# Two pads shift the upper half of the on-chip memory map so that matmul operands start at multiples of 128 bytes

## The chip, the cores and the metric

The kernel runs on one core of a Trainium2 chip. The metric is the device time of one execution in microseconds (us). The kernel before takes 2042.87 us, the median of 3 runs (2042.85 to 2042.97).

## The reference

Three layers follow each other; each one's output is the next one's input.

```
# attention: softmax of q over the head dimension, of k over the sequence
kv = einsum('bhsd,bhse->bhde', softmax_seq(k), v)          # 4 batches, 8 heads, 576 x 64
x  = einsum('bhsd,bhde->bhse', softmax_dim(q), kv)         # -> 2304 tokens x 512
# first MLP, float64 weights
h = x @ w_in; x = maximum(0.01*h, h) @ w_out               # 512 -> 2048 -> 512
# eight experts, every token through all of them
P = exp(x @ w_gate - max); 8 rounds of row and column normalization   # 2304 x 8
out = sum_e P[:, e] * (maximum(x @ w1[e], 0) @ w2[e])      # 512 -> 1024 -> 512
```

## The kernel before

**Numbers.** Matmul operands of the two MLPs are float32 values kept as two `fp32r` parts, a high one and a low one. Each product is three matmuls, high*high, high*low, low*high, summed in PSUM. The helper `mm` (line 178 in the profile) issues them all. Every matmul is paired with its own weight load: one operand (the second argument of `mm`, the stationary one, 128 x 128) is loaded into the array by LDWEIGHTS, the other (the third argument, the moving one, 384 or 512 columns) is streamed through it.

**First MLP** (functions `first` and `second`): four phases `ph` of 24 steps each, six token blocks of 384 by four weight units. One step is a `first` (tile `ph`, 12 matmuls of 384 columns: stationary weights, moving `xs`) and a `second` (tiles `y0` to `y3`, 12 matmuls of 384 columns: stationary weights, moving `hh`). In phases 0 and 2 the weights lie in tile `wa`, in phases 1 and 3 in tile `wb_t`. After a block's fourth unit, VectorE adds `y` into `acc` (line 217); the next `second` writes the same PSUM banks. Attention work is interleaved into the time before the first MLP and into its phase 0.

**Experts** (functions `group`, `product`, `y_tile`): 96 groups. Each runs seven products of six matmuls with 384 columns (tiles `pa` to `pd`: stationary `wa`, moving `xs`), and three output tiles of 12 matmuls with 512 columns (tile `e`: stationary the hidden activations, which lie in `xs`; moving the second weights, which lie in `wb_t`). The first two groups have no output tiles, and two more after the last group have nothing else, so there are 96 sets of 36 such matmuls.

**What sets the order.** Python code writes out the order of all engines (a manual schedule with the tables at `at(...)`); the change touches none of it.

**Where tiles lie.** Tiles are placed one behind the other, every size rounded up to 32 bytes per partition. Pools on the left grow upward from byte 16512, which follows a scratch area and four small constants. Pools with `side="right"` grow downward from byte 229344. The table gives the start of each tile that a matmul reads, as the allocation places it, per partition, before and after the change:

| tile | read by | bytes | start before | mod 128 | start after | mod 128 |
|---|---|---|---|---|---|---|
| `ident`, `ones` | attention transposes, column sums | 512 | 16512, 17024 | 0 | same | 0 |
| `acc` (6) | attention | 6144 | 18816 and on | 0 | same | 0 |
| `xs` | moving in `ph`, `p*`; stationary in `e` | 79872 | 55680 | 0 | same | 0 |
| `wa` | stationary in `ph`, `y`, `p*` | 32768 | 135552 | 0 | same | 0 |
| `hh` (2) | moving in `y` | 3072 | 168416, 171488 | 96 | 168448, 171520 | 0 |
| `wb_t` | stationary in `ph`, `y`; moving in `e` | 32768 | 196576 | 96 | 196480 | 0 |
| `kv` (2) | attention | 2048 | 200288, 202336 | 96 | 200192, 202240 | 0 |
| `k`, `v`, `ke` | attention | 2304, 2560, 2560 | 204384 and on | 96 | 204288 and on | 0 |

Inside these tiles every operand starts at a multiple of 128 bytes from the tile's start, except the gate's weights in `wa` (48 matmuls, in steps of 64 bytes). Besides, 19 small matmuls of the balancing stage read `mrow`, `mall` and `cs`, which start at other multiples of 32 before and after. Tiles that no matmul reads move too: `raw`, `pair`, `ca` and `s` from 32 to 64 mod 128, the small attention and balance statistics by 32 or 96 bytes, and `g`, `c1`, `c2` with `hh` from 96 to 0.

The 96 comes from `mrow`, `mall` and `mneg`: three tiles of 4 bytes in pool `const`, 32 bytes each, in front of pool `h`. On the right side the pools hang from 229344, which is itself 96 mod 128.

Of the kernel before, what the change touches and what calls it, by code (L numbers as in the profile page):

```python
# [8 lines left out]
F32 = mybir.dt.float32  # L9
# [6 lines left out]
P = 128  # L16
# [6 lines left out]
def kernel(  # L23
# [51 lines left out]
    const = ctx.enter_context(tc.tile_pool(name="const", bufs=1))  # L75
# [23 lines left out]

    wa = const.tile([P, PU * US], F32R, name="wa")  # L100

    ml = ml_ctx.enter_context(tc.tile_pool(name="ml", bufs=2))
    att = att_ctx.enter_context(tc.tile_pool(name="att", bufs=2, side="right"))

# [697 lines left out]
```

## Time and profile before

| what | value |
|---|---|
| median of 3 runs | 2042.87 us |
| profiled execution: its time | 2042.97 us |
| its span, first to last instruction | 2041.2 us |
| TensorE (PE) matmul busy | 2007.7 us, 98% |
| weight loads (PEld) busy | 1824.1 us, 89% |
| VectorE (DVE) busy | 1294.8 us, 63% |
| ScalarE (ACT) busy | 806.2 us, 39% |
| GpSimd (POOL) busy | 485.9 us, 24% |
| matmul instructions | 10323 |

The time outside the span is 2042.97 - 2041.2 = 1.77 us. In the span, attention alone fills about the first 55 us, the first MLP runs to about 521 us (phase 0 to about 190, phases 1, 2 and 3 of about 105 to 125 us), and the experts take the rest. The granted clock of TensorE has a mean of 0.992 of full speed. A matmul's duration in the profile is longer than its pitch, the distance from its start to the next one's start, because matmuls are pipelined: durations of successive matmuls overlap. Where matmuls follow without a wait, the pitch is what the time is made of.

### The profile page before, as it was taken

What the parts mean: (1) busy time and instruction counts of PE and PEld (TensorE: products, weight loads), DVE (VectorE), ACT (ScalarE), POOL (GpSimd) and SP (SyncE); (2) the same over time, 40 slices, a digit from 0 to 9 for tenths busy, and PEclk for the clock granted to TensorE, in tenths of its full rate; (3) what the DMA queues carried; (4) which work ended last, traced back from release to release, by engine and by line L of the source; (5) the groups of instructions that cost most, each with busy time, mean ns of one, the idle gap of its engine ahead of it and who ended that gap; (6) DMA issues with size and microseconds to landing.
All of it is one profiled execution on the core that took longest, in us unless ns stands there. A gap on an engine that the chain in (4) does not pass through costs nothing.

```text
span 2041.2 us, 26341 instructions
## 1 busy us (share of the span) xinstructions
PE 2007.7 (98%) x10323; PEld 1824.1 (89%) x10323; DVE 1294.8 (63%) x1941; ACT 806.2 (39%) x1367; POOL 485.9 (24%) x476
## 2 busy tenths in 40 slices
PE   6999999999999999999999999999999999999999
PEld 5899999998889889988998899889888988898887
DVE  8746534335786666666766666666686666666663
ACT  6654323224443333333444333333344333333331
POOL 2324313200223223122132231221322312313220
PEclk8999999999999999999999999999999999999999
DMA  6502111100212212112132122121212221212210
GB/s 228 175 1 83 43 41 42 52 1 0 83 42 83 83 42 83 67 58 83 42 114 83 42 83 69 56 83 44 80 64 92 83 75 50 83 49 76 83 42 31
DMA packets 65452, 138.55 MB, mean 68 GB/s; under 512 B 4656, under 2 KB 4656, under 8 KB 65328
## 3 DMA queue, kind: packets, MB, share of 16 engines
q1 hardware_dynamic: 65328, 136.87, 19.5%
q8 instruction: 81, 1.33, 0.3%
q14 instruction: 43, 0.35, 0.1%
HBM read 132.14 MB, written 4.72 MB: 67 GB/s over the span
## 4 chain that ended last, share of the span: by engine, by line
PE 73%; DVE 1%; ACT 0%; issue 0%; DVEq 0%; ACTq 0%
PE e L178 39%; PE pc L178 10%; PE pd L178 10%; PE pa L178 10%; PE pb L178 5%; DVE wa L446 0%; PE y L178 0%; DVE xs L555 0%; ACT wa L445 0%; DVE pm L387 0%; DVE cs L388 0%; PE pt L178 0%; PE pcs L178 0%; PE pg L178 0%; DVE rs L386 0%; DVE rs L384 0%
## 5 line engine op out<-in xcount | busy, mean ns | idle before, releaser
L178 PE MATMUL e<-wb_t,xs 128*128 128x512 f32 x3456 | 822.4, 395 | 0.0
L178 PEld LDWEIGHTS e<-wb_t,xs 128*128 128x128 f32 x3456 | 647.3, 188 | 148.6
L452 POOL TENSOR_TENSOR s<-pair 128x256 f32<-128x256 f32 x96 | 73.8, 769 | 1207.2 <-DMA pair<-in_w 631.6
L548 DVE SCALAR_TENSOR_TENSOR acc<-e,pm,acc 128x512 f32<-128x512 f32 x264 | 193.2, 744 | 105.7 <-PE e L178 103.0
L178 PE MATMUL pa<-xs,wa 128*128 128x384 f32 x1152 | 231.9, 335 | 0.0
L555 DVE SCALAR_TENSOR_TENSOR xs<-c,xs 128x384 fp32r<-128x384 f32 (+1 forms) x192 | 185.8, 986 | 72.6 <-ACT xs L554 72.6
L178 PE MATMUL pc<-xs,wa 128*128 128x384 f32 x1152 | 230.8, 334 | 0.0
L178 PE MATMUL pd<-xs,wa 128*128 128x384 f32 x1152 | 230.6, 334 | 0.0
L554 ACT ACTIVATE xs<-c 128x768 fp32r<-128x768 f32 x192 | 126.7, 681 | 242.0 <-PE e L178 221.5
L178 PEld LDWEIGHTS pa<-xs,wa 128*128 128x128 f32 x1152 | 203.3, 188 | 8.5
L178 PEld LDWEIGHTS pd<-xs,wa 128*128 128x128 f32 x1152 | 202.4, 188 | 0.1
L178 PEld LDWEIGHTS pc<-xs,wa 128*128 128x128 f32 x1152 | 202.4, 188 | 0.2 <-issue 0.2
L196 DVE TENSOR_TENSOR hh<-g,hh 128x384 fp32r<-128x384 f32 x96 | 58.7, 611 | 208.3 <-ACT g L195 208.3
L446 DVE TENSOR_TENSOR wa<-s,wa 128x768 fp32r<-128x768 f32 x96 | 91.9, 957 | 101.7 <-ACT wa L445 101.6
L445 ACT CAST wa<-s 128x768 fp32r<-128x768 f32 x96 | 80.2, 835 | 168.8 <-POOL s L455 148.2
L570 DVE TENSOR_TENSOR c<-c 128x384 f32<-128x384 f32 x96 | 54.2, 564 | 134.4 <-ACT c L590 134.4
L580 ACT COPY c<-pa 128x384 f32<-128x384 f32 x96 | 46.1, 480 | 212.3 <-PE pa L178 196.9
L194 ACT ACTIVATE hh<-ph 128x384 fp32r<-128x384 f32 x96 | 47.2, 491 | 191.0 <-PE y L178 180.3
L446 DVE TENSOR_TENSOR wa<-pair,wa 128x1024 fp32r<-128x1024 f32 x96 | 120.8, 1258 | 2.6 <-ACT wa L445 2.5
L446 DVE TENSOR_TENSOR wb_t<-pair,wb_t 128x1024 fp32r<-128x1024 f32 x96 | 114.1, 1224 | 8.5 <-PE y L178 4.7
L178 PE MATMUL y<-hh,wb_t 128*128 128x384 f32 x576 | 111.8, 343 | 4.5 <-DVE acc L217 4.2
L455 POOL TENSOR_TENSOR s<-pair,s 128x256 f32<-128x256 f32 x96 | 114.2, 1190 | 7.5
(117 smaller groups left out, 2519.5 us busy)
## 6 DMA issues: line engine op xcount, KB each, us to landing
pair<-in_w SPq DMA_DIRECT2D x192, 512.0 KB, 5.0
raw<-in_wm SPq DMA_DIRECT2D x32, 512.0 KB, 3.8
v<-in_vt SPq DMA_DIRECT2D x16, 320.0 KB, 5.3
k<-in_kt SPq DMA_DIRECT2D x16, 288.0 KB, 5.5
out<-acc SPq DMA_DIRECT2D x18, 256.0 KB, 2.0
acc<-in_q SPq DMA_DIRECT2D x5, 768.0 KB, 6.1
acc<-in_q SPq DMA_DIRECT2D x3, 256.0 KB, 6.8
wg_t<-in_wg SPq DMA_DIRECT2D x1, 16.0 KB, 5.3
```

What stands on the lines that cost most here:

```text
L178: nc.tensor.matmul(o, a, b, start=start, stop=stop, **more)
L194: nc.scalar.activation(hh[:, 0, :], p, AF.Prelu, alpha=0.01)
L196: nc.vector.tensor_tensor(hh[:, 1, :], g, r32(hh[:, 0, :]), op=ALU.subtract)
L445: nc.scalar.copy(hi, a)
L446: return lambda: nc.vector.tensor_tensor(lo, a, r32(hi), op=ALU.subtract)
L452: nc.gpsimd.tensor_tensor(s[:, 0], a21, a22, op=ALU.add)
L455: nc.gpsimd.tensor_tensor(s[:, 2], a12, s[:, 1], op=ALU.subtract)
L548: nc.vector.scalar_tensor_tensor(a, y, scale, a, op0=ALU.mult, op1=ALU.add)
L554: nc.scalar.activation(o[:, 0], p, AF.Relu)
L555: nc.vector.scalar_tensor_tensor(o[:, 1], p, 0.0, r32(o[:, 0]), op0=ALU.max, op1=ALU.subtract)
L570: add = lambda o, x, y: nc.vector.tensor_tensor(o, x, y, op=ALU.add)
L580: nc.scalar.copy(c1, bk[0])
```

## The change

Two tiles are allocated that nothing reads or writes. `pad`, 8 floats or 32 bytes, is added to pool `const`, whose total becomes a multiple of 128 bytes with it. `rpad`, 24 floats or 96 bytes, lies in a pool of its own at the top of the right side, so that all other pools there start 96 bytes lower, at 229248. No instruction is added, removed or moved on any engine or queue, and no wait changes; only start addresses in instructions and DMAs differ, as in the table above.

```diff
     wa = const.tile([P, PU * US], F32R, name="wa")
 
+
+    const.tile([P, 8], F32, name="pad")
+    ctx.enter_context(tc.tile_pool(name="rpad", bufs=1, side="right")).tile(
+        [P, 24], F32, name="rpad"
+    )
     ml = ml_ctx.enter_context(tc.tile_pool(name="ml", bufs=2))
     att = att_ctx.enter_context(tc.tile_pool(name="att", bufs=2, side="right"))
```

## Rows read from the trace of the kernel before

**Rows 1.** The page's first part: the span, and TensorE's busy time
```profile
span 2041.2 us, 26341 instructions
...
PE 2007.7 (98%) x10323; PEld 1824.1 (89%) x10323; DVE 1294.8 (63%) x1941; ACT 806.2 (39%) x1367; POOL 485.9 (24%) x476
```

**Rows 2.** The page's chain that ended last: shares by engine
```profile
PE 73%; DVE 1%; ACT 0%; issue 0%; DVEq 0%; ACTq 0%
```

**Rows 3.** Stretches: us, busy per engine, PEclk, DMA share, GB/s; phase 0, then experts
```profile
55.00:190.00 135.00, 133.96 (x803) 127.98 (x803) 82.20 (x164) 76.74 (x175) 44.88 (x36) 0.99 0.23 78
...
600.00:1000.00 400.00, 400.00 (x1988) 357.55 (x1987) 266.03 (x361) 152.24 (x230) 98.85 (x104) 1.00 0.20 69
```

**Rows 4.** Groups on PE, 600 to 2012 us: count | busy, mean ns | idle before
```profile
L178 PE MATMUL e<-wb_t,xs 128*128 128x512 f32 x3241 | 770.9, 395 | 0.0
L178 PE MATMUL pd<-xs,wa 128*128 128x384 f32 x1086 | 217.3, 334 | 0.0
```

**Rows 5.** Timeline of PE, one expert group: start us, us, instructions merged, count
```profile
1487.21 1.20 PE L178 MATMUL pa<-xs,wa 128*128 128x384 f32 x6
...
1494.49 8.56 PE L178 MATMUL e<-wb_t,xs 128*128 128x512 f32 x36
1502.89 1.20 PE L178 MATMUL pa<-xs,wa 128*128 128x384 f32 x6
```

**Rows 6.** Tiles e and pa, 600 to 2012 us: duration ns min/median/max
```profile
L178 PE MATMUL e<-wb_t,xs x3241: 391/394/400, 600.7 to 2011.9; 128*128 128x512 f32 x191
...
L178 PE MATMUL pa<-xs,wa x1080: 333/334/335, 609.1 to 2009.7; 128*128 128x384 f32 x180
```

**Rows 7.** Timeline of PE, first MLP, from phase 1 into phase 2
```profile
293.85 2.25 PE L178 MATMUL ph<-xs,wa 128*128 128x384 f32 x12
295.94 2.25 PE L178 MATMUL y<-hh,wb_t 128*128 128x384 f32 x12
298.02 2.25 PE L178 MATMUL ph<-xs,wa 128*128 128x384 f32 x12
```

**Rows 8.** Timeline of PE, first MLP, four steps of phase 2
```profile
319.33 2.27 PE L178 MATMUL ph<-xs,wa 128*128 128x384 f32 x12
321.67 2.35 PE L178 MATMUL y<-hh,wa 128*128 128x384 f32 x12
...
325.95 2.28 PE L178 MATMUL y<-hh,wa 128*128 128x384 f32 x12
328.07 2.27 PE L178 MATMUL ph<-xs,wa 128*128 128x384 f32 x12
330.18 2.28 PE L178 MATMUL y<-hh,wa 128*128 128x384 f32 x12
...
336.52 2.27 PE L178 MATMUL ph<-xs,wa 128*128 128x384 f32 x12
```

**Rows 9.** Timeline of PE, first MLP, four steps of phase 1
```profile
216.68 2.28 PE L178 MATMUL ph<-xs,wb_t 128*128 128x384 f32 x12
...
221.19 2.28 PE L178 MATMUL ph<-xs,wb_t 128*128 128x384 f32 x12
223.31 2.25 PE L178 MATMUL y<-hh,wb_t 128*128 128x384 f32 x12
225.40 2.28 PE L178 MATMUL ph<-xs,wb_t 128*128 128x384 f32 x12
...
233.81 2.28 PE L178 MATMUL ph<-xs,wb_t 128*128 128x384 f32 x12
```

**Rows 10.** Timeline of PE, phase 3: two waits [idle before <-releaser]
```profile
484.65 3.67 PE L178 MATMUL y<-hh,wb_t 128*128 128x384 f32 x12 [1.86 <-DVE acc L217]
...
508.50 3.63 PE L178 MATMUL y<-hh,wb_t 128*128 128x384 f32 x12 [2.35 <-DVE acc L217]
```

**Rows 11.** Stretches, columns as in rows 3: after a wait; VectorE's fullest group
```profile
485.00:495.00 10.00, 9.63 (x47) 8.75 (x46) 6.85 (x9) 4.32 (x7) 0.00 (x0) 0.83 0.01 2
...
1515.68:1531.36 15.68, 15.68 (x80) 14.04 (x79) 15.68 (x20) 7.87 (x11) 3.92 (x4) 1.00 0.22 83
```

**Rows 12.** Groups on DVE, 600 to 2012 us, columns as in rows 4
```profile
L446 DVE TENSOR_TENSOR wa<-pair,wa 128x1024 fp32r<-128x1024 f32 x89 | 111.2, 1249 | 0.0
L446 DVE TENSOR_TENSOR wb_t<-pair,wb_t 128x1024 fp32r<-128x1024 f32 x90 | 106.7, 1224 | 0.6 <-ACT wb_t L445 0.6
```

## The prediction

> **What bounds the kernel now.** I read the page's first part, then the chain, then stretches, then PE's timeline. TensorE's matmuls fill 98% of the span [rows 1], and 73% of the chain that ended last is PE [rows 2]. An average hides stages, so the stretches come next: PE is busy for 133.96 of 135 us in phase 0, and for all of 400 us of the experts, with every other engine well below it [rows 3]. In the experts no matmul sat idle at all [rows 4]. So there the time is the number of matmuls times their pitch, and a change that shortens the pitch by some ns counts in full. This change can act in no other way: it moves addresses alone.
>
> So the question is whether the pitch depends on where operands start. The trace holds its own comparison, because some tiles start at 0 mod 128 and some at 96.
>
> In the experts the seven products have both operands at 0 (`wa`, `xs`). They take from 1487.21 to 1494.49, 7.28 us for 42 matmuls: 173.3 ns for 384 columns, 0.4514 ns a column [rows 5]. The output tiles have the stationary operand at 0 (`xs`) and the moving one at 96 (`wb_t`). They take from 1494.49 to 1502.89, 8.40 us for 36: 233.3 ns for 512 columns, 0.4557 ns a column [rows 5]. At the products' rate it would be 0.4514 x 512 = 231.1 ns. The durations say the same in another way. All products have 333 to 335 ns, while the output tiles range over 391, 394 and 400 [rows 6], so some matmuls have 6 ns too much, which for one in three makes the 2 ns of difference.
>
> Two column counts are a weak comparison; the first MLP has the better one, with 12 matmuls of 384 columns throughout. From phase 1 into 2, `ph` from `wa` (0 and 0) takes 293.85 to 295.94, 2.09 us, and `y` with `hh` and `wb_t` (96 and 96) takes 2.08 us [rows 7]. In phase 2, `y` with `hh` at 96 and `wa` at 0 takes 325.95 to 328.07, 2.12 us, and the `ph` after it 2.11 [rows 8]. In phase 1, `ph` with `wb_t` at 96 and `xs` at 0 takes 2.12 us, and the `y` after it (96 and 96) 2.09 [rows 9]. So a block is short where both operands have one residue mod 128, whichever it is, and 0.03 us longer where the two differ. A `ph` with equal residues is 0.02 us longer when it follows a block with unequal ones [rows 8], and not when it follows an equal one [rows 7]. I read it as the two reads, of the next weights and of the moving columns, getting in each other's way when they are out of step. That is inferred from the rows, not shown.
>
> **The change part by part.** It removes and adds no instruction. After it every operand of these matmuls is at 0, the case of the products.
>
> Output tiles of the experts: 36 x 231.1 = 8.32 us in place of 8.40, 0.08 us for each of 96 sets: 7.7 us. No row shows 512 columns with equal residues, so here are the bounds. At most the pitch stays: 0. At least, it is 384 columns plus a constant: at full clock (2.4 GHz) 384 columns are 160 ns, and 173.3 leaves 13.3; 512 columns are 213.3, with the same constant 226.7, a set 8.16 us, 0.24 x 96 = 23 us. I take the proportional value, because two of the three durations (391, 394) already stand near it.
>
> First MLP, phase 2: four steps take 319.33 to 336.52, 17.19 us [rows 8]. After the change each `y` takes 2.09, four of them 8.36, and three `ph` 6.27. The first `ph` of a block is followed by a wait. The `y` after it begins 2.34 us after the `ph` before it began [rows 8], since VectorE must first add the last `y` into `acc`; this is a delay from the end of that `y`, so what `ph` gains there is swallowed. With 0.07 us for the longer first `y` that comes to 8.36 + 6.27 + 2.34 + 0.07 = 17.04, 0.15 less, and six blocks give 0.9 us.
>
> Phases 1 and 3: four steps take 216.68 to 233.81, 17.13 us [rows 9]. Only `ph` is slow here, and three of four count: 3 x 0.03 x 6 = 0.5 us a phase, 1.0 us for both.
>
> Phase 0 has 24 `y` at 0.03 = 0.7 us and up to 0.4 of the `ph` behind them; the attention work between them hides nothing, as PE is busy [rows 3]. Bounds 0 and 1.1; I take 0.6.
>
> Phase 3 has two waits of 1.86 and 2.35 us for VectorE [rows 10]. A PE that comes earlier waits longer there, which swallows something between 0 and phase 3's 0.5. I take 0.2 off. Behind each wait the clock is lower (0.83 in the mean [rows 11]) and a block's merged length is 3.67 instead of 2.25 us: 1.4 us each. The waits get longer by some hundredths, so both drops stay. If they vanished it would be -2.8 us, and one more +1.4; both ends are kept for the range.
>
> What I cost at nothing: attention before 55 us, where other engines set the pace, 0 to 0.5 us. Starts of tiles that only VectorE, ScalarE, GpSimd and DMAs touch: VectorE writes `wa` (at 0) in 1249 ns and `wb_t` (at 96) in 1224 ns, from the same tile [rows 12], a difference of 2% and the other way round. The cover is that PE does not wait for VectorE even in its fullest group, 15.68 busy of 15.68 us [rows 11]; were it gone, 2% of that is 0.3 us in each of the two such transitions between token blocks.
>
> Sum: 7.7 + 0.9 + 1.0 + 0.6 - 0.2 = 10.0 us from the profiled execution's 2042.97, which stands 0.1 above the median: 2033.0 us, and against the median 2032.9.
>
> A rule of the Trainium skill speaks against all this. The page "TensorE: Matmul & The Clock Gate", section "Step-by-step: what each phase is for", says that TensorE reads through two independent ports, so that loading the next weights takes nothing from the running matmul. The page "SBUF — State Buffer", section "Specifications (TRN2)", gives lines of 16 bytes; 96 and 0 are both whole lines. By either the change does nothing, and the time is 2042.9. The trace does not agree: 2.12 against 2.09 us for the same 12 matmuls [rows 7 to 9].
>
> **The rivals.**
> A, no change: the longer pitch belongs to something other than the residue. For it: in the output tiles all 36 matmuls have the same residues, yet the durations vary between 391 and 400 [rows 6], and stationary tile, order of parts and column count differ from the products as well. Against it: `y` and `ph` each come in both kinds with the same code and column count, and the slow one is always the unequal one [rows 7 to 9]. Time 2042.9. The two rules above end here. Chance 9%.
>
> B, more gain: the constant of 13.3 ns, 512 columns at 226.7. For it: two column counts cannot tell a rate from a constant. Against it: no duration in 3241 is below 391, 9 less than the longest, while this needs a mean 6.6 below the present pitch. 2042.9 - 23 - 2.3 = 2017.6. Chance 4%.
>
> C, slower: equal residues suit 384 columns, but with 512 the two reads meet in every matmul, and the 6 ns that one in three has now falls on all three. Place: the output tiles. Price: 2 x 1152 matmuls x 6 ns = 13.8 us, less the 2.3 of the first MLP: 2054.4. For it: a `ph` with both operands at 0 also takes 2.11 us in places [rows 8]. Against it: 1080 `pa` with both at 0 never do [rows 6]. It decides from a set above 8.40 + 2.3 / 96 = 8.42 us. Chance 3%.
>
> **How the numbers follow.** The forecast has 84%; its own range, from the terms' bounds and one clock drop either way, is 2030.5 to 2036. The range of 8 in 10 is 2030 to 2037.5; it leaves out A, B and C, 16 in 100, and little of the forecast. A measurement of this kernel can tell 0.2%, 4.1 us, from no change: faster means below 2038.8. Faster: 84 + 4 = 88%, of which I move 1 to same, for a gain that stays under 4.1 because the output tiles give less than a quarter of theirs. Same: 10%. Slower: 3%.
>
> **What would show it.** A set of 36 output matmuls in 8.32 us, `e` durations within 2 ns of each other, `pa` unchanged at 334. `y` in phase 2 and `ph` in phase 1 in 2.09 us, and `ph` after `y` in phase 2 in 2.09 throughout. The experts' period of 7.28 + 8.40 us would become 15.60. It is wrong if the set stays at 8.40, or if it shortens while the blocks of the first MLP do not, for then the residue is not the cause; if PE shows idle time in the experts; or if the clock drops behind other waits than the two in phase 3.

## The result and the profile after

The changed kernel takes 2024.98 us, the median of 5 runs (2024.35 to 2026.04), against 2042.87 before (5 runs, 2040.18 to 2043.03): a ratio of 0.9917 with a 95% interval of 0.9905 to 0.9929. Forecast were 2033.0 and a range of 2030.0 to 2037.5. The direction was right, the gain of 18 us was nearly twice the 10 us of the sum.

The page's first part, against [rows 1]: the span shrinks by 18.0 us and PE's busy time by 18.4, while the busy times of the other engines move by at most 2.1 us.

```profile
span 2023.2 us, 26341 instructions
...
PE 1989.3 (98%) x10323; PEld 1824.9 (90%) x10323; DVE 1294.1 (64%) x1941; ACT 806.0 (40%) x1367; POOL 488.0 (24%) x476
```

PE's timeline of one expert group, against [rows 5]. A row gives the start, the merged length from the first start to the last end, and the count; what a group of matmuls takes is read from its start to the start of the next row. The second row is the view of a window that opens inside the set of the first, and so holds its last 24 matmuls alone:

```profile
1482.90 8.36 PE L183 MATMUL e<-wb_t,xs 128*128 128x512 f32 x36
...
1485.66 5.60 PE L183 MATMUL e<-wb_t,xs 128*128 128x512 f32 x24
1491.10 1.23 PE L183 MATMUL pa<-xs,wa 128*128 128x384 f32 x6
1492.16 1.20 PE L183 MATMUL pb<-xs,wa 128*128 128x384 f32 x6
...
1498.40 8.36 PE L183 MATMUL e<-wb_t,xs 128*128 128x512 f32 x36
```

The 36 output matmuls of a group, called a set below, take 8.20 us in place of 8.40, and the period is 15.50 in place of 15.68. The first 12 come every 230 ns (1482.90 to 1485.66), the last 24 every 226.7 (1485.66 to 1491.10). The `pa` behind them takes 1.06 in place of 1.04. Durations (min/median/max), against [rows 6], and the idle time of the groups, against [rows 4]:

```profile
L183 PE MATMUL e<-wb_t,xs x3237: 387/389/398, 599.7 to 1987.1; 128*128 128x512 f32 x191
...
L183 PE MATMUL pa<-xs,wa x1074: 333/334/346, 607.2 to 1988.2; 128*128 128x384 f32 x179
```
```profile
L183 PE MATMUL e<-wb_t,xs 128*128 128x512 f32 x3237 | 752.0, 390 | 0.0
```

The median of `e` fell from 394 to 389, but its spread did not close, and some `pa` now last 346. PE still waits for nothing here. The first MLP, phase 1 and then phase 2, against [rows 9] and [rows 8]:

```profile
219.50 2.24 PE L183 MATMUL ph<-xs,wb_t 128*128 128x384 f32 x12
221.59 2.28 PE L183 MATMUL y<-hh,wb_t 128*128 128x384 f32 x12
223.70 2.24 PE L183 MATMUL ph<-xs,wb_t 128*128 128x384 f32 x12
...
317.74 2.25 PE L183 MATMUL ph<-xs,wa 128*128 128x384 f32 x12
...
322.30 2.25 PE L183 MATMUL ph<-xs,wa 128*128 128x384 f32 x12
324.38 2.28 PE L183 MATMUL y<-hh,wa 128*128 128x384 f32 x12
326.50 2.24 PE L183 MATMUL ph<-xs,wa 128*128 128x384 f32 x12
...
334.90 2.25 PE L183 MATMUL ph<-xs,wa 128*128 128x384 f32 x12
```

A block is the 12 matmuls of one `ph` or one `y`. `ph` from `wb_t` went from 2.12 to 2.09 as forecast. But `y` from `wa` stayed at 2.12, and `y` from `wb_t` rose from 2.09 to 2.11. Four steps of phase 2 take 17.16 us (317.74 to 334.90), where 17.04 was forecast. The waits of phase 3, against [rows 10]; the `pt` at 1.30 us of idle comes right at the first MLP's end, here in the changed kernel and then in the kernel before:

```profile
482.88 3.89 PE L183 MATMUL y<-hh,wb_t 128*128 128x384 f32 x12 [1.89 <-DVE acc L222]
...
506.99 3.89 PE L183 MATMUL y<-hh,wb_t 128*128 128x384 f32 x12 [2.43 <-DVE acc L222]
...
517.78 0.27 PE L183 MATMUL pt<-wa 16*128 16x8 f32 x1 [1.30 <-ACT wa L358]
```
```profile
519.26 0.27 PE L178 MATMUL pt<-wa 16*128 16x8 f32 x1 [1.30 <-ACT wa L353]
```

So 1.5 of the 18.0 us lie before the experts and 16.5 in them: 96 x (0.20 - 0.025) = 16.8, with the `pa` rise of 0.025 taken from its single starts. Of the 1.5, 0.9 are there when phase 0 starts (54.14 against 55.06). That is less than executions of one layout differ by: two traces of one kernel, `all384` and `all384_b` below, start it at 53.59 and 54.92, and the kernel before, with only its output matmuls split (`split_before` below), starts it at 53.29. The first row is of the kernel before, the second of `split_before`:

```profile
55.06 6.03 PE L178 MATMUL ph<-xs,wa 128*128 128x384 f32 x24
```
```profile
53.29 6.23 PE L178 MATMUL ph<-xs,wa 128*128 128x384 f32 x24
```

The first MLP itself gave 0.6 us, that is 0.7 and 0.1 less in phases 0 and 2, and 0.05 and 0.2 more in phases 1 and 3.

### The profile page after: what moved, and what is told of

Same layout as the page of the kernel before. It is cut to its first block, busy times and chain, and to the rows that moved or that the text cites. A ratio compares the mean times of both kernels' runs of the same rounds, so it can differ in the third digit from the quotient of the medians.

```text
span 2023.2 us, 26341 instructions
## 1 busy us (share of the span) xinstructions
PE 1989.3 (98%) x10323; PEld 1824.9 (90%) x10323; DVE 1294.1 (64%) x1941; ACT 806.0 (40%) x1367; POOL 488.0 (24%) x476
## 4 chain that ended last, share of the span: by engine, by line
PE 73%; DVE 1%; ACT 0%; issue 0%; ACTq 0%; DVEq 0%
PE e L183 38%; PE pa L183 10%; PE pc L183 10%; PE pd L183 10%; PE pb L183 5%; DVE wa L451 0%; PE y L183 0%; DVE xs L560 0%; ACT wa L450 0%; DVE pm L392 0%; DVE cs L393 0%; PE pcs L183 0%; PE pt L183 0%; PE pg L183 0%; DVE rs L391 0%; DVE rs L389 0%
## 5 line engine op out<-in xcount | busy, mean ns | idle before, releaser
L183 PE MATMUL e<-wb_t,xs 128*128 128x512 f32 x3456 | 803.4, 390 | 0.0
```

What stands on the lines that cost most here:

```text
L183: nc.tensor.matmul(o, a, b, start=start, stop=stop, **more)
```

## The experiments

The forecast rested on equal residues mod 128. The trace after fits neither that nor the change's own words in full: all operands are at 0 mod 128, and `y` is slow. In the finer residues a pattern shows: mod 512, `xs`, `wa` and `wb_t` now lie at 384 and `hh` at 0; before, `hh` and `wb_t` lay at 480. Two theories follow. R: a matmul's pitch is at its floor, the shortest that it can have, where stationary and moving operand have the same residue, mod 512 or mod 256. M: multiples of 128 are what counts. All edits are shown against the changed kernel, with `...` for what is left out, and only start addresses differ, up to the split. Where no range or count stands beside a time, it is that of one execution; the kernel before took 2042.73 to 2043.13 us beside these runs. Such a time also holds the first MLP, which took 461.55 and 459.54 us in two traces of one kernel (`all384` and `all384_b`), so the sets are what to compare.

**One pad at a time.** `left_only`:

```diff
-    ctx.enter_context(tc.tile_pool(name="rpad", bufs=1, side="right")).tile(
-        [P, 24], F32, name="rpad"
-    )
```

> The left pad alone (32 bytes): hh moves from 96 to 0 mod 128, wb_t stays at 96. Theory R (residues mod 512): the pitch is at its floor where the two operands of a matmul start at the same residue mod 512 and longer where they differ; before, wa and xs are at 384, hh and wb_t at 480. Theory M (multiples of 128): the pitch is at its floor where both operands start at a multiple of 128 bytes. Both expect the 36 output matmuls of an expert group to stay at 8.40 us, so a time within 2 us of the kernel before. R expects y from wb_t (hh now at 0, wb_t at 480, no longer equal) to get longer than its 2.08 to 2.09 us a block, and y from wa (0 against 384) to be no shorter than 2.09. M expects y from wa at 2.085.

`right_only`:

```diff
-    const.tile([P, 8], F32, name="pad")
```

> The right pad alone (96 bytes): wb_t at 0 mod 128 and at 384 mod 512 as wa and xs, hh stays at 96 (480 mod 512). Theories R and M both expect the output matmuls of the experts at 8.20 us for 36, as with both pads, so 2024 to 2028 us, nearly all of the gain, and ph from wb_t at 2.08 to 2.10 us. R expects y from wb_t (480 against 384, no longer equal) to rise from 2.09 to 2.12 and y from wa to stay at 2.12. M expects y at 2.12 in both phases too. A rival on hh, that the left pad carries the gain, expects 2042.

Measured: 2038.81 and 2024.68 us. The set and the `pa` after it, left pad alone and then right pad alone:

```profile
1490.31 8.56 PE L179 MATMUL e<-wb_t,xs 128*128 128x512 f32 x36
1498.71 1.20 PE L179 MATMUL pa<-xs,wa 128*128 128x384 f32 x6
```
```profile
1482.59 8.36 PE L181 MATMUL e<-wb_t,xs 128*128 128x512 f32 x36
1490.80 1.23 PE L181 MATMUL pa<-xs,wa 128*128 128x384 f32 x6
```

8.40 and 8.21: the right pad, which moves `wb_t`, carries the gain. `left_only` is 4 us faster all the same, where at most 2 were expected; 1.8 of that is its earlier start of phase 0 (53.30 us), about 1.4 is a clock drop of phase 3 that this execution does not show (behind an idle of 1.89 us its block is 2.32 long, not 3.67), the rest lies in the blocks of the first MLP, none in the experts. In `right_only`, `ph` from `wb_t` takes 2.11, not the 2.08 to 2.10 expected, though its operands are equal; the `y` before it has unequal ones. In one more point R missed. First MLP, left pad alone:

```profile
219.28 2.25 PE L179 MATMUL ph<-xs,wb_t 128*128 128x384 f32 x12
221.37 2.24 PE L179 MATMUL y<-hh,wb_t 128*128 128x384 f32 x12
223.45 2.24 PE L179 MATMUL ph<-xs,wb_t 128*128 128x384 f32 x12
```

`y` at +32 and `ph` at -96 (moving minus stationary) both take 2.08 to 2.09, though unequal, and this `ph` at -96 took 2.12 before. So at 384 columns a difference does not always cost; what ran before it matters too.

**Equal residues, aligned and not.** `all384` puts `hh` on the residue of the others, `equal32` shifts everything by 32 bytes besides:

```diff
 # all384
-    const.tile([P, 8], F32, name="pad")
+    const.tile([P, 104], F32, name="pad")
```
```diff
 # equal32: all384, and
+    const.tile([P, 8], F32, name="pre")      # ahead of ident
...
-        [P, 24], F32, name="rpad"
+        [P, 16], F32, name="rpad"
```

> The left pad is 416 bytes in place of 32, the right pad stays at 96, so that hh too starts at 384 mod 512, as xs, wa and wb_t do. In the changed kernel hh is at 0 mod 512 and y repeats pitches of 181, 176, 173, 174, 175 ns, 2.10 us a block. R expects all pitches of y at 173 to 174 ns, 2.085 us a block, and 1.5 to 2.5 us less than the changed kernel: about 2023. M expects no difference from the changed kernel, 2025, with the pattern of five kept.

> Everything lies 32 bytes higher than in the run with hh at 384: xs, wa, hh and wb_t all start at 416 mod 512, so at 32 mod 128; none of these operands is at a multiple of 128 any more, but all are at one residue. R expects the same time as there, 2023, with 36 output matmuls in 8.20 us. M expects the gain gone or worse: 8.40 us or more for the 36, 2043 or more.

Measured: 2023.09 us (4 runs, 2020.53 to 2024.22) and 2023.94 (4 runs, 2020.34 to 2024.18), ratios to before 0.9904 (0.9889 to 0.9919) and 0.9904 (0.9888 to 0.9921). In the traces of both, every block of phases 1 and 2 that holds no wait takes 2.08 us. In `equal32`, where no such operand is at a multiple of 128, the set is as short:

```profile
1481.75 8.36 PE L183 MATMUL e<-wb_t,xs 128*128 128x512 f32 x36
1489.95 1.23 PE L183 MATMUL pa<-xs,wa 128*128 128x384 f32 x6
```

M falls: what the pads gave is not alignment but agreement of two addresses.

**How wide the agreement must be.** `off256` and `m128`:

```diff
 # off256
-    const.tile([P, 8], F32, name="pad")
+    const.tile([P, 40], F32, name="pad")
...
-        [P, 24], F32, name="rpad"
+        [P, 88], F32, name="rpad"
```
```diff
 # m128
-        [P, 24], F32, name="rpad"
+        [P, 56], F32, name="rpad"
```

> hh and wb_t both at 128 mod 512 (left pad 160 bytes, right pad 352), wa and xs at 384: multiples of 128 bytes everywhere, 256 apart where a matmul takes one of each. Theory R with modulus 512: the 36 output matmuls of an expert group take more than 8.20 us (8.25 to 8.45), y from wa and ph from wb_t more than 2.08 us, y from wb_t (equal) 2.08. Theory R with modulus 256: 8.20 and 2.08 everywhere, 2023. Theory M (multiples of 128): as with the two pads of the change, 8.20.

> hh at 0 and wb_t at 256 mod 512 (left pad 32, right pad 224 bytes), wa and xs at 384: still multiples of 128 everywhere, but the moving operand of the output matmuls lies 128 below the stationary one. M expects 8.20 us for 36 and the time of the changed kernel, 2025. R with a modulus of 256 or 512 expects 8.25 to 8.45, so 2030 to 2045.

Measured: 2022.65 and 2041.89 us. The sets of `off256` and `m128`:

```profile
1480.57 8.36 PE L182 MATMUL e<-wb_t,xs 128*128 128x512 f32 x36
1488.77 1.23 PE L182 MATMUL pa<-xs,wa 128*128 128x384 f32 x6
```
```profile
1493.18 8.56 PE L182 MATMUL e<-wb_t,xs 128*128 128x512 f32 x36
1501.58 1.21 PE L182 MATMUL pa<-xs,wa 128*128 128x384 f32 x6
```

8.20 at 256 apart, 8.40 at 128 apart: the modulus is 256. `m128` has every operand at a multiple of 128 and loses the whole gain of the experts.

**Other differences.** `p32`, `m32` (with `hh` moved by 64 besides), then `wb_t` or `wa` alone by 64 or 96:

| run | `pad`, floats | `rpad`, floats | other |
|---|---|---|---|
| `p32` | 120 | 16 | |
| `m32` | 88 | 32 | |
| `wb_p64` | 104 | 8 | |
| `wb_m64` | 104 | 40 | |
| `wb_m96` | 104 | 48 | |
| `wa_p64` | 88 | 24 | `const.tile([P, 16], F32, name="mid")` ahead of `wa` |

> wb_t 32 bytes above the residue of wa and xs (416 against 384 mod 512), hh 64 above (448); so output matmuls and y from wb_t have the moving operand 32 above the stationary one, ph from wb_t 32 below, y from wa 64 above. R in its strict form (only equal residues reach the floor) expects 36 output matmuls between 8.25 and 8.40 us and all blocks of 12 with wb_t or hh above 2.09. A looser form, S (a difference costs only where the two reads come to collide, and some differences do not), expects 8.16 to 8.20 and 2.08 for the +32 pairs, since y from wb_t at +32 took 2.079 us in the run with the left pad alone.

> The mirror image: wb_t 32 bytes below wa and xs (352 against 384 mod 512), hh 64 below (320): output matmuls and y from wb_t have the moving operand 32 below the stationary one, ph from wb_t 32 above, y from wa 64 below. R expects 8.25 to 8.40 us for 36 output matmuls. S expects that the sign matters: if +32 is free and -32 is not, 8.25 or more here and 8.20 there, or the other way round.

> wb_t alone 64 bytes above the residue of xs, wa and hh (448 against 384 mod 512). Theory R256 (the floor needs equal residues mod 256, as the run at 256 apart showed): 36 output matmuls at 8.3 to 8.4 us like the other unequal ones (8.39 to 8.40 at +32, -32, +96 and 128), time about 2040. Theory P64 (differences of 64 are free too, as y from wa at +64 and -64 took 2.075 and 2.076 us): 8.16 to 8.20 and 2018 to 2023 us, and perhaps without the longer first matmuls that the equal residues show when the stream changes between pa to pd and e.

> wb_t alone 64 bytes below the residue of xs, wa and hh (320 against 384 mod 512). R256: 8.3 to 8.4 us for 36 output matmuls, about 2040. P64: 8.16 to 8.20, 2018 to 2023.

> wb_t alone 96 bytes below the residue of xs, wa and hh (288 against 384 mod 512), the opposite sign of the kernel before. R256 and P64 both expect 8.3 to 8.4 us for 36 output matmuls and about 2040; a theory by which only the sign of the difference matters expects 8.20.

> wa alone 64 bytes above the residue of xs, hh and wb_t (448 against 384 mod 512). This puts the difference into the products pa to pd and ph (stationary wa) and leaves the output matmuls equal. R256: the products rise from 1.04 us for six to 1.05 to 1.07, that is 7 x 96 x 0.01 to 0.03 = 7 to 20 us, so 2029 to 2043. P64: products stay at 1.04, output matmuls at 8.16 to 8.20, 2018 to 2025.

The sets of `p32`, `m32`, `wb_p64` and `wb_m96`:

```profile
1491.05 8.56 PE L182 MATMUL e<-wb_t,xs 128*128 128x512 f32 x36
1499.45 1.22 PE L182 MATMUL pa<-xs,wa 128*128 128x384 f32 x6
```
```profile
1491.43 8.55 PE L182 MATMUL e<-wb_t,xs 128*128 128x512 f32 x36
1499.82 1.23 PE L182 MATMUL pa<-xs,wa 128*128 128x384 f32 x6
```
```profile
1484.64 8.41 PE L182 MATMUL e<-wb_t,xs 128*128 128x512 f32 x36
1492.89 1.22 PE L182 MATMUL pa<-xs,wa 128*128 128x384 f32 x6
```
```profile
1481.26 8.59 PE L182 MATMUL e<-wb_t,xs 128*128 128x512 f32 x36
1489.69 1.23 PE L182 MATMUL pa<-xs,wa 128*128 128x384 f32 x6
```

| run | moving minus stationary in `e`, mod 256 | set of 36, us | time, us |
|---|---|---|---|
| after, `all384`, `equal32`, `off256`, `right_only` | 0 | 8.20 | 2022.65 to 2024.98 |
| `wb_p64` | +64 | 8.25 | 2028.47 |
| `m32` | -32 | 8.39 | 2040.60 |
| `wb_m64` | -64 | 8.40 | 2038.88 |
| `p32` | +32 | 8.40 | 2040.19 |
| before, `left_only` | +96 | 8.40 | 2042.87, 2038.81 |
| `m128` | 128 | 8.40 | 2041.89 |
| `wb_m96` | -96 | 8.42 | 2047.35 |

Only equality reaches the short set. R's figure for +64 (8.3 to 8.4) and P64's (8.16 to 8.20) both missed; P64 missed at -64 as well, S at +32 and -32, and the sign alone decides nothing. At -96 the set and the time lie a little above what every theory gave. At 384 columns the strict form of R does not hold: `y` from `wa` at +64 (`p32`) and -64 (`m32`) takes 2.08 us, as with equal operands. `wa_p64` (2024.78) puts 64 between the products' operands:

```profile
1489.80 1.21 PE L183 MATMUL pa<-xs,wa 128*128 128x384 f32 x6
1490.85 1.21 PE L183 MATMUL pb<-xs,wa 128*128 128x384 f32 x6
...
1497.13 3.15 PE L183 MATMUL e<-wb_t,xs 128*128 128x512 f32 x13
```

Its products rise to 1.04 to 1.05, in R's direction; but the seven of them take 7.33 us where the changed kernel has 7.30 (1491.10 to 1498.40, above), some 3 us in 96 groups, so its time is P64's and R priced this too high.

**What a matmul costs.** `split_equal` (on `all384`) and `split_before` (on the kernel before) issue each output matmul as two of 256 columns:

```diff
+        for ns in (slice(0, 256), slice(256, 512)):
...
-                mm(y, hh, w2(i)[:, 0, u], beg, False)
+                    mm(y[:, ns], hh, w2(i)[:, 0, u, ns], beg, False)
...
```

> As the run with hh at 384 mod 512 (all operands at one residue), but each output matmul of 512 columns is issued as two of 256, first the 12 of the left half, then the 12 of the right: 72 matmuls a group in place of 36. It sizes what failed in the prediction. If a matmul costs its columns at full clock plus a constant of 13.3 ns (160 + 13.3 for 384, 213.3 + 13.3 for 512), 256 columns take 120.0 ns and a set 8.64 us, so 0.44 x 96 = 42 us more than unsplit: 2065. If it costs 0.4514 ns a column, as the prediction took it, 256 columns take 115.6 ns and a set 8.32 us: 2034.

> The same split in the kernel before (wb_t 96 above xs mod 256). Against the floor of 226.7 ns its 512-column matmuls are 6.7 ns too long. If unequal residues cost something per matmul, 256 columns take 120 + 6.7 = 126.7 ns and a set 9.12 us; if they cost per column streamed, 120 + 3.3 = 123.3 and 8.88 us. With the proportional rate of the prediction 115.6 plus either.

Measured: 2061.78 and 2065.15 us.

```profile
1488.90 8.79 PE L182 MATMUL e<-wb_t,xs 128*128 128x256 f32 x72
1497.53 1.21 PE L182 MATMUL pa<-xs,wa 128*128 128x384 f32 x6
```
```profile
1492.12 8.80 PE L178 MATMUL e<-wb_t,xs 128*128 128x256 f32 x72
1500.77 1.20 PE L178 MATMUL pa<-xs,wa 128*128 128x384 f32 x6
```

8.63 us for 72 is 119.8 ns each: the constant, not the rate. In `split_before` it is 8.65, 120.1 ns: at 256 columns the difference of 96 costs nothing in the mean, which neither reading had. The floors of 120.0, 173.3 and 226.7 ns at 256, 384 and 512 columns lie on one line: 2.4 columns a ns, which is full clock, plus 13.3 ns. Over it the difference of 96 costs 0 at 256 columns, up to 3.3 at 384 (2.12 us / 12 = 176.7), 6.7 at 512 (233.3).

**Does agreement everywhere beat the change?** `all384_b` and `two_pads` are `all384` and the changed kernel again, unedited, on one chip.

> The run with hh at 384 mod 512 again, now beside the changed kernel on one chip, to tell whether it beats it: the blocks of the first MLP are 0.01 to 0.04 us shorter, of which 72 steps give 2 to 3 us less waits; expected 1 to 3 us under the changed kernel, if the clock drops in phase 3 do not cover it.

> The changed kernel itself, for the comparison with the run with hh at 384 mod 512: 2024.4 to 2026.0 as measured.

Measured: 2020.82 us (4 runs, 2020.17 to 2022.01) against 2026.31 (5 runs, 2024.22 to 2026.80); ratios to before 0.9892 (0.9878 to 0.9905) and 0.9916 (0.9902 to 0.9930). It beats the change in every run, by more in the medians than the 1 to 3 us expected. Its first MLP, phase 2, and one wait of phase 3; then the stretch that holds this wait (columns as in [rows 3]), in the changed kernel and in `all384_b`:

```profile
313.09 2.24 PE L182 MATMUL ph<-xs,wa 128*128 128x384 f32 x12
315.17 2.24 PE L182 MATMUL y<-hh,wa 128*128 128x384 f32 x12
...
317.25 2.25 PE L182 MATMUL ph<-xs,wa 128*128 128x384 f32 x12
...
334.29 1.03 PE L182 MATMUL ph<-xs,wa 128*128 128x384 f32 x5
```
```profile
481.19 2.35 PE L182 MATMUL y<-hh,wb_t 128*128 128x384 f32 x12 [1.90 <-DVE acc L221]
```
```profile
480.00:490.00 10.00, 7.85 (x35) 6.82 (x33) 7.95 (x12) 3.70 (x6) 0.00 (x0) 0.83 0.01 2
...
480.00:490.00 10.00, 8.21 (x46) 7.35 (x47) 8.39 (x12) 4.10 (x7) 0.00 (x0) 1.00 0.01 2
```

Every block without a wait takes 2.08 us, four steps 17.04 in place of the 17.16 of the changed kernel: about 2 us over the 18 token blocks of phases 1 to 3. The clock adds 1.5 in this trace: behind the first wait the block is 2.35 long, not 3.89, and the granted clock is 1.00 (2.4 GHz) through the ten us in which the changed kernel has 0.83 in the mean, a part of it at 1.2 GHz. So in this execution that drop did not come, at the same idle time. It comes and goes with the execution: of the 18 traces of this document, 8 show no drop behind the first wait (blocks of 2.32 to 2.36, idle 1.86 to 1.90 us) and 10 show one; `all384` shows it and `all384_b`, the same kernel, does not. What decides it is open. The profiled pair is 2.9 us apart, the medians 5.5; the other executions of the two have no trace, so what makes up the difference is not shown. In its first runs `all384` led by 2 us.

## Why the prediction was wrong

**What bounds the kernel, and where the change acts: right.** PE idles nowhere in the experts, and shorter pitches counted in full.

**The step that failed is the size of the output tiles' term, "36 x 231.1 = 8.32 us".** The choice between a rate per column and columns plus a constant was made for the rate, because durations of 391 and 394 stood near it. The runs show the constant: 120 ns at 256 columns, 173.3 at 384 and, past a set's first matmuls, 226.7 at 512. All three durations of [rows 6] carried some of the cost: in the changed kernel the median is 389, and every matmul past the first twelve of a set lasts 389. The term was 7.7 us and measured 96 x 0.20 = 19 us. It had the constant as its bound (23 us) and as rival B with 4%: B had the size right, and 2017.6 was too low by what the next two points tell. That the forecast's direction came out owes something to luck: `wb_t` and `xs` were put at 0 mod 128, and only by chance at one residue mod 256; `m128` has the same multiples of 128 and gains nothing in the experts.

**Missing from the sum: the change of stream.** With equal residues the first nine or so matmuls of a set come at 224 to 236 ns, a set of 8.20 where 36 x 226.7 = 8.16, and the `pa` behind it is 0.025 longer: 2.4 us given back in `pa` alone. The kernel before showed nothing of it. Equality is not its condition: in `m32`, `p32` and `wb_m96`, all unequal, the `pa` behind a set is 0.02 to 0.03 longer too. Why the stream takes that long to settle is open.

**The first MLP: right idea, wrong modulus.** "Equal residues" held, but mod 256 and not mod 128. `hh` at 0 against `wa` and `wb_t` at 128 is unequal, so `y` gained nothing in phases 0 and 2 and lost in 1 and 3. Forecast 2.3 us, measured 0.6. Phase 0 alone came near its term (0.7 for 0.6), but 0.6 of it lies in the `ph` and 0.1 in the `y`, which were to give most. The forecast's own sign of being wrong was there: the set shortened, the `y` blocks did not. With all operands equal mod 256, `all384_b` does take the 17.04 us for four steps of phase 2 that the forecast worked out. `off256`, `m128` and `all384` show the modulus. [rows 7 to 9] could not: 96 and 0 differ under both.

**Clock drops: right in the result, not in the reason.** Both waits grew (1.86 to 1.89, 2.35 to 2.43) and both drops stayed, but the blocks behind them lengthened to 3.89, which is why phase 3 lost 0.2 us. That a longer wait keeps the drop is not borne out: behind 1.90 us of idle in `all384_b` there is none, so in this trace it could have gone either way.

**Costed at nothing: right** for tiles that no matmul reads; `equal32` moves them all and changes no block. Rival A fell with the result, and rival C too: no set of the changed kernel grew.

**The two independent read ports** that the Trainium skill states ("TensorE: Matmul & The Clock Gate", section "Step-by-step: what each phase is for") do not make the pitch independent of how the two start addresses stand to each other. Shifting the moving operand alone by 32 bytes (`p32`) takes a set from 8.20 to 8.40 us, shifting both (`equal32`) leaves it at 8.20. Nor do the 16-byte lines of the Trainium skill ("SBUF — State Buffer", section "Specifications (TRN2)") explain it, since all shifts are multiples of 32. That the weight load of the next matmul and the stream of the running one disturb each other is what this argues for; it is not shown, and neither is the part of the memory in which it would happen. The load records do not tell the cases apart: a weight load of `e` lasts 187 to 188 ns before and after.

## What to carry to other kernels

Where fp32r matmuls of 384 or 512 columns, each with its own weight load, run back to back, compare the start addresses of stationary and moving operands with each other, mod 256, and not with a boundary; a pad of some 100 bytes was worth 0.8% here. Before pricing a pitch from two column counts, ask which of a rate and a constant a third count would show, and keep the larger one in the range if the rows cannot tell. A pad placed for one pair can separate another (`hh` and `wb_t` here), so list every pair first.

## What was not expected of the hardware

- Unequal residues mod 256 cost 2 ns (+64) to 7 ns (-96) a matmul at 512 columns over the pitch of 226.7, and 0 to 3.3 at 384; the one difference tried at 256 columns, 96, cost nothing.
- The cost comes in a pattern that repeats: the pitches of a set go 232, 238, 231 ns over and over in the kernel before, 238, 229 in `m128`, and 231, 235, 233, 234 in `p32`.
- The cost is not a function of the difference alone: at 384 columns, -96 took 2.12 us a block after one neighbour and 2.09 after another.
- The fixed part of an fp32r matmul with its own weight load is 13.3 ns at 256, 384 and 512 columns alike.
- After an idle of 1.89 us the granted clock dropped in one execution (a block of 3.89 us merged length), after 1.90 us in another it did not (2.35). Behind the second wait (2.32 to 2.51 us) it dropped in 16 of 18 traces.
